# Windowed attention and rational hidden layer on one core: the early part written anew

## The chip, the cores and the metric

The kernel runs on 1 core of one Trainium2 chip. The metric is the time of one execution on the device in microseconds (us); the time before is the median of three runs.

## The reference

```python
def _attn_ref(x, weight_gen):            # x 4 x 4096 x 192, weight_gen 4 x 4096 x 8 x 7
    w = weight_gen - np.max(weight_gen, axis=-1, keepdims=True)
    w = np.exp(w)
    w = w / (np.sum(w, axis=-1, keepdims=True) + 1e-09)
    ...
    out = np.einsum('bshk,bskhg->bshg', w, x_unf)

def _moe_ref(x, w_in, w_out, a, b):      # w_in 192 x 2048, w_out 2048 x 192
    h = x @ w_in
    h2 = h * h
    h3 = h2 * h
    P = a[0] + a[1] * h + a[2] * h2 + a[3] * h3
    Q = 1.0 + np.abs(b[0]) * np.abs(h) + np.abs(b[1]) * h2
    g = P / (Q + 1e-06)
    return (g @ w_out).astype(np.float32)
```

Each token has, for each of 8 heads, seven softmaxed weights over itself and the six tokens before it (the taps). The weighted sum, 192 wide, goes through a hidden layer of 2048 with the rational function g = P/Q. The inputs `w_in` and `w_out` come as 64-bit numbers, which the kernel rounds to 32 bits itself.

## The kernel before

The 16384 tokens are cut into 32 chunks of 512 (128 partitions, 4 tokens each). A chunk is prepared: loads of the gates and of x (`lg`, `lx`), the softmax (L509 to L534), seven taps, each a product x times weight (L560) with a sum, four or six transposes on PE (`tr`), a rounding to the product's number format (`cast`, ScalarE), the residue of that rounding (`rest`, VectorE), and copies with the partitions' halves swapped by DMA (`both`, xd L680 and xs L686). For all chunks but the first, POOL multiplies and adds the taps (L560, L572, L578). For chunk 0 (`early`) VectorE multiplies all seven, PE adds them in PSUM by products with an identity (`fold`, L596), ScalarE and VectorE copy the sum out (`settle` L603, `again` L608), and xs alone comes by DMA.

A chunk then has 8 slots of 256 hidden numbers each, 256 slots in all, counted through. A slot is: `m1`, the product on PE into an `h` tile (L716, 18 matmuls of high and low parts of weights and tokens); `v1`, Abs, and `z1`, Square of it on ScalarE (L750, L754); `d1` and `w1` on VectorE (L758, L762), the denominator and a factor of the numerator; `ln` and `ex` on ScalarE (L767, L770), which together invert the denominator; `gg` on VectorE (L774); and `m2` on PE, the sum over hidden numbers into the chunk's output tile `acc`, in two halves of 8 matmuls (L729; rows of the trace count 16, since each appears as two parts). Between the halves stands `relay`, an empty instruction on SP (L791): the second half waits for it, and it for the end of the first. After a chunk's last slot ScalarE copies `acc` out (L829) and SP issues the store (L832). There is one `acc`, so the next chunk's first half waits for that copy.

The weights come in 14 units (A0 to A3 and B0, B1 of `w_in`, W0 to W7 of `w_out`): a DMA (`ul`), an Abs of the high words and a rounding of the low words on ScalarE (`ua1` L397, `ua2` L401), four operations on VectorE that put the 32-bit number together (`ub1` to `ub4`, L406 to L421), of which the last sets to zero what is smaller in size than `TINY`; for A and B also a rounding on ScalarE and its residue on VectorE (`uh` L449, `uw` L452). Slot i of chunk 0 or 1 needs A(i//2), B(i//4) for its product and Wi for its sum.

The coefficients a and b come by two broadcast DMAs on ScalarE's queue (L264, L265); POOL, ScalarE and VectorE work two roots out of them (L279, L285 to L296), `powers` and `vertex` the numbers that the slots use. `judge` (POOL) tests the bounds within which this form of g may be used; if `slow` comes out as 1, the kernel computes all once more by `whole`. 30 products of the identity with itself (L274, `warm`) stand at the start of PE.

The order on each engine is not that of the code: every step is an `Op` with an engine, a duration, a key and what it needs, and `arrange` plays the schedule through and puts the instruction that can start with the smallest key next. Keys are due times, slot number times `PITCH` plus offsets `OFF` by kind of step, and `KEY` for the weight units.

```python
    def due(n):
        return START + PITCH * n
...
        o_d = op("DVE", 1.28, end - OFF["d"], d1, [o_v], uses=[AV], lock=True)
```

## Time and profile before

| | us |
|---|---|
| median of 3 runs (lowest, highest) | 1295.23 (1294.98, 1295.98) |
| profiled execution, its own time | 1295.15 |
| its span | 1293.4 |
| PE matmul busy in the span | 1249.6 (97%) |
| PEld, weight load of PE | 1150.7 (89%) |
| DVE (VectorE) | 1135.3 (88%) |
| ACT (ScalarE) | 1130.5 (87%) |
| POOL (GpSimd) | 883.1 (68%) |

The span goes from the first to the last recorded instruction; what lies around it is 1.75 us here. PEld overlaps PE. SP (SyncE) issues DMAs and relays and has no busy time of its own. A shape such as 128x1024 is partitions by elements. A row by stretch gives the engines in the order PE, PEld, DVE, ACT, POOL, then the clock granted to PE as a share of full speed, the DMA engines' busy share and GB/s.

### The profile page before, as it was taken

How to read it: one execution, taken by the hardware profiler on the slowest of the kernel's cores; microseconds unless marked ns; L12 is line 12 of the kernel's file. 1: busy time of each engine (PE TensorE's matmuls, PEld its weight loads, DVE VectorE, ACT ScalarE, POOL GpSimd, SP SyncE). 2: the span in 40 equal slices, each digit the busy share in tenths (PEclk: the TensorE clock that was granted, in tenths of full speed). 3: DMA queues.
4: the chain of work that ended last, by engine and by line, in shares of the span. 5: the costliest groups of instructions: out<-in, count | busy, mean ns of one | idle time of the engine just before them, and what ended most of it. 6: DMA issues, size and time to landing. Idle time of an engine off the chain costs nothing.

```text
span 1293.4 us, 31029 instructions
## 1 busy us (share of the span) xinstructions
PE 1249.6 (97%) x13268; PEld 1150.7 (89%) x13268; DVE 1135.3 (88%) x979; ACT 1130.5 (87%) x1162; POOL 883.1 (68%) x578
## 2 busy tenths in 40 slices
...
DMA packets 46293, 89.11 MB, mean 69 GB/s; under 512 B 5426, under 2 KB 27976, under 8 KB 46148
## 3 DMA queue, kind: packets, MB, share of 16 engines
...
q8 instruction: 106, 1.74, 0.5%
...
## 4 chain that ended last, share of the span: by engine, by line
PE 84%; DVE 5%; ACT 4%; POOL 3%; issue 2%; SPq 1%; DMA 1%; DVEq 0%; ACTq 0%; POOLq 0%
PE acc L729 47%; PE h L716 37%; ACT av L750 1%; DMA x<-in_x_dram 1%; ACT av L767 1%; DVE av L758 1%; POOL at L572 1%; ACT av L770 1%; DVE g L774 1%; POOL pr L560 1%; ACT pv L754 1%; PE h L644 1%; SPq L686 1%; SPq L680 0%; DVE h L411 0%
## 5 line engine op out<-in xcount | busy, mean ns | idle before, releaser
L729 PE MATMUL acc<-wo,g 64*128 64x192 f32 x8192 | 721.9, 324 | 13.5 <-DVE g L774 5.4
L729 PEld LDWEIGHTS acc<-wo,g 64*128 64x128 f32 x8192 | 683.9, 187 | 37.4 <-SPq L791 12.0
L758 DVE SCALAR_TENSOR_TENSOR av<-av,cf 128x1024 f32<-128x1024 f32 x256 | 422.5, 1650 | 97.6 <-ACT av L750 97.0
L572 POOL TENSOR_TENSOR at<-at,pr 128x768 f32<-128x768 f32 x155 | 362.9, 2341 | 12.0
L774 DVE SCALAR_TENSOR_TENSOR g<-h,ab,av 128x1024 f32<-128x1024 f32 x256 | 326.8, 1276 | 31.5 <-ACT av L770 22.5
L750 ACT ACTIVATE av<-h 128x1024 f32<-128x1024 f32 x256 | 260.9, 1019 | 83.3 <-PE h L716 82.5
L560 POOL TENSOR_TENSOR pr<-x,wn 128x768 f32<-128x768 f32 x186 | 332.7, 1789 | 0.1
L762 DVE SCALAR_TENSOR_TENSOR h<-pv,cf,h 128x1024 f32<-128x1024 f32 x256 | 326.3, 1274 | 2.2 <-ACT pv L754 2.2
L767 ACT ACTIVATE av<-av,c 128x1024 f32<-128x1024 f32 x256 | 294.1, 1149 | 32.3 <-DVE av L758 31.3
L754 ACT ACTIVATE pv<-h,cf,rt 128x1024 f32<-128x1024 f32 x256 | 307.7, 1202 | 0.0
L770 ACT ACTIVATE av<-av 128x1024 f32<-128x1024 f32 x256 | 270.6, 1057 | 2.8
L716 PE MATMUL h<-xm,wh 64*128 64x512 f32 x1024 | 242.1, 461 | 16.2 <-DVE g L774 13.8
L716 PE MATMUL h<-xs,wh 64*128 64x512 f32 x1024 | 208.9, 394 | 1.6 <-DMA xs<-xm 1.6
L716 PE MATMUL h<-xd,wh 64*128 64x512 f32 x1024 | 208.2, 394 | 0.0
L716 PEld LDWEIGHTS h<-xm,wh 64*128 64x128 f32 x1024 | 102.3, 188 | 27.7 <-issue 6.9
L716 PEld LDWEIGHTS h<-xs,wh 64*128 64x128 f32 x1024 | 102.6, 187 | 21.5 <-DMA xs<-xm 2.9
L716 PEld LDWEIGHTS h<-xd,wh 64*128 64x128 f32 x1024 | 102.0, 187 | 18.7
L513 POOL TENSOR_TENSOR e<-wgt,mx 128x224 f32<-128x224 f32 x31 | 20.9, 674 | 140.0 <-DVE mx L509 127.1
L716 PE MATMUL h<-xs,wl 64*128 64x512 f32 x512 | 104.2, 393 | 0.0
L716 PE MATMUL h<-xd,wl 64*128 64x512 f32 x512 | 103.9, 393 | 0.0
L716 PE MATMUL h<-xm,wl 64*128 64x512 f32 x512 | 103.9, 393 | 0.0
L578 POOL TENSOR_TENSOR as<-at,pr 128x512 f32<-128x512 f32 (+1 forms) x62 | 84.4, 1379 | 2.3
...
## 6 DMA issues: line engine op xcount, KB each, us to landing
...
```

What stands on the lines that cost most here:

```text
L560: eng.tensor_tensor(dst.rearrange("p q (h g) -> p q h g", g=G), t["x"][:, k:k + Q, :].rearrange("p q (h g) -> p q h g", g=G), t["wn"][:, k ...
L572: eng.tensor_tensor(at, at, term, op=ALU.add)
L578: eng.tensor_tensor(t["as"][:, start:start + Q * (hi - lo)].rearrange("p (q d) -> p q d", q=Q), at[:, :, lo:hi], term[:, :, lo:hi], op=ALU ...
L716: nc.tensor.matmul(h[:, f, :], w[half, b_, i, :], v[half, part, 0:N], start=k == 0, stop=k == 8, skip_group_check=True)
L729: done.append(nc.tensor.matmul(acc[:, bank, q_ * D:(q_ + 1) * D], g[half, f, seat(q) * P:(seat(q) + 1) * P], wo[half, 2 * i + f, :], start ...
L750: nc.scalar.activation(out=t["v"], in_=flat(t["h"]), func=ACTF.Abs)
L754: nc.scalar.activation(out=t["z"], in_=flat(t["h"]), func=ACTF.Square, scale=steep, bias=shift)
L758: nc.vector.scalar_tensor_tensor(out=t["v"], in0=t["v"], scalar=rb, in1=t["v"], op0=ALU.add, op1=ALU.mult)
L762: nc.vector.scalar_tensor_tensor(out=flat(t["h"]), in0=t["z"], scalar=lift, in1=flat(t["h"]), op0=ALU.add, op1=ALU.mult)
L767: nc.scalar.activation(out=t["v"], in_=t["v"], func=ACTF.Ln, bias=c0)
L770: nc.scalar.activation(out=t["v"], in_=t["v"], func=ACTF.Exp, scale=-1.0)
L774: nc.vector.scalar_tensor_tensor(out=flat(t["g"]), in0=flat(t["h"]), scalar=a0, in1=t["v"], op0=ALU.add, op1=ALU.mult)
```

## The change

- **Weight mask.** The units lose the Abs on ScalarE (`ua1`) and the masking on VectorE (`ub4`). Instead each unit is loaded a second time later (`verify`, from slot 40 on, one unit per chunk): an Abs on ScalarE, a compare-and-multiply and a maximum on VectorE. At the end one maximum over all goes to `slow`; if any weight is small and not zero, `whole` follows, after the weights have been masked as before (`refill`).
- **Squares on ScalarE.** For slots 0 to 6 (`SQUARED`) the step `d1`, v(v + rb) on VectorE, becomes (v + rb/2) squared on ScalarE (`q1`, in place), with the constant put right in the bias of `ln`. `judge` has a further bound on rb/2.
- **Swapped copy of chunk 0.** xs comes from four more transposes, a rounding and a residue (`trs`, `casts`, `rests`) in place of a DMA.
- **Taps of chunk 0.** The fifth and sixth are multiplied and summed on POOL (`few`, `pair`, `join`), the other five on VectorE; x is issued before the first weights.
- **Coefficients.** They come to one partition by two short DMAs and are spread by a product with a row of ones (`spread`) and a copy.
- **Dummy products.** 24 in place of 30 at the start, and `fill` puts groups of them in gaps of over 1.2 us that the planner sees on PE before 75 us; each group waits for one vector or scalar operation (`after`). The groups hold 52 in all.
- **Planner.** New numbers in `OFF`, `KEY`, `PITCH`, `PATIENCE`, `LOCK`, and with them another order on all engines over the whole program.

ScalarE where the first slots begin; `av`, `pv` and `h` are tiles of a slot, `cf` and `c` coefficients, `raw` and `rnd` belong to a weight unit. L750 is now L907, L754 L911, L767 L927, L770 L931; L919 is `q1`. Before:

```order
L750 ACTIVATE av<-h 128x1024
L754 ACTIVATE pv<-h,cf,rt 128x1024
L750 ACTIVATE av<-h 128x1024
L767 ACTIVATE av<-av,c_68 128x1024
L770 ACTIVATE av<-av 128x1024
L754 ACTIVATE pv<-h,cf,rt 128x1024
L767 ACTIVATE av<-av,c_68 128x1024
L770 ACTIVATE av<-av 128x1024
```

And now:

```order
L907 ACTIVATE av<-h 128x1024
L911 ACTIVATE pv<-h,cf,rt 128x1024
L907 ACTIVATE av<-h 128x1024
L911 ACTIVATE pv<-h,cf,rt 128x1024
L919 ACTIVATE av<-av,cf 128x1024
L927 ACTIVATE av<-av,cf 128x1024
L931 ACTIVATE av<-av 128x1024
L466 ACTIVATE rnd<-raw 128x512
L466 ACTIVATE rnd<-raw 128x384
L919 ACTIVATE av<-av,cf 128x1024
L927 ACTIVATE av<-av,cf 128x1024
L931 ACTIVATE av<-av 128x1024
```

The `ln` of slot 0 (L927) now follows a square on the same engine where it followed a step of VectorE, and two roundings of weights (L466, before L401) have moved between the two slots.

VectorE around the taps of chunk 0 (L560, now L666), with weight operations L406 to L421 (now L471 to L482). Before:

```order
L406 TENSOR_SCALAR h<-raw 128x512
L411 SCALAR_TENSOR_TENSOR h<-raw,h 128x512
L416 ISA h<-h,rnd 128x1024
L560 TENSOR_TENSOR pr<-x,h 128x768 x4
L406 TENSOR_SCALAR h<-raw 128x512
L560 TENSOR_TENSOR pr<-x,h 128x768 x2
L421 SCALAR_TENSOR_TENSOR h<-mag,h 128x512
L560 TENSOR_TENSOR pr<-x,h 128x768
```

And now:

```order
L347 RECIPROCAL tt<-rt 128x1
L348 SCALAR_TENSOR_TENSOR rt<-tt,sq,rt 128x1
L350 TENSOR_SCALAR rt<-rt 128x1
L351 RECIPROCAL tt<-rt 128x1
L666 TENSOR_TENSOR pr<-x,h 128x768 x4
L471 TENSOR_SCALAR h<-raw 128x512
L476 SCALAR_TENSOR_TENSOR h<-raw,h 128x512
L482 ISA h<-h,rnd 128x1024
L666 TENSOR_TENSOR pr<-x,h 128x768
L505 TENSOR_TENSOR wl<-h,wh 128x512
```

The second root's four operations (L347 to L351) now stand ahead of the taps, and the first weight unit's behind four of them.

PE where chunk 4 begins (slot 32): `acc` is a chunk's output tile, `wo` the output weights, `g` a slot's values, and L716 (now L873) the product of one slot. Before:

```order
L729 MATMUL acc_2311<-wo_71,g_2219 128x192 x8
L716 MATMUL h_2326<-xm_1867,wh_69 128x512 x2
L716 MATMUL h_2326<-xm_1867,wl_70 128x512 x2
L716 MATMUL h_2326<-xm_1867,wh_69 128x512 x2
L716 MATMUL h_2326<-xd_1900,wh_69 128x512 x2
L716 MATMUL h_2326<-xd_1900,wl_70 128x512 x2
L716 MATMUL h_2326<-xd_1900,wh_69 128x512 x2
L716 MATMUL h_2326<-xs_1905,wh_69 128x512 x2
L716 MATMUL h_2326<-xs_1905,wl_70 128x512 x2
L716 MATMUL h_2326<-xs_1905,wh_69 128x512 x2
L729 MATMUL acc_2311<-wo_71,g_2219 128x192 x8
L729 MATMUL acc_2311<-wo_71,g_2261 128x192 x8
```

And now:

```order
L886 MATMUL acc_1897<-wo_75,g_2168 128x192 x8
L873 MATMUL h_2363<-xm_1939,wh_73 128x512 x2
L873 MATMUL h_2363<-xm_1939,wl_74 128x512 x2
L873 MATMUL h_2363<-xm_1939,wh_73 128x512 x2
L873 MATMUL h_2363<-xd_1974,wh_73 128x512 x2
L873 MATMUL h_2363<-xd_1974,wl_74 128x512 x2
L873 MATMUL h_2363<-xd_1974,wh_73 128x512 x2
L873 MATMUL h_2363<-xs_1979,wh_73 128x512 x2
L873 MATMUL h_2363<-xs_1979,wl_74 128x512 x2
L873 MATMUL h_2363<-xs_1979,wh_73 128x512 x2
L886 MATMUL acc_2388<-wo_75,g_2219 128x192 x16
L886 MATMUL acc_2388<-wo_75,g_2272 128x192 x8
```

The product before stood between the two halves of the new chunk's first slot (acc_2311, g_2219); it now stands between the old chunk's last half (acc_1897) and the first of the new, and the two halves of that slot, x16, follow each other as a pair.

The diff, cut to its core (left out: the number tables, helpers that only moved, the second computation):

```diff
+CHECKED = 40
+SQUARED = 7
...
-PATIENCE = 0.302
+PATIENCE = 0.222
...
+def fill(order, filler):
+    done, last = [], None
+    gates = [o for o in order if o.eng in ("DVE", "ACT") and o.start < FILLED]
+    at = {o: i for i, o in enumerate(order)}
+    extra = {}
+    for o in order:
+        if o.eng != "PE":
+            continue
+        if last is not None and o.start < FILLED and o.start - last.end > 1.2:
+            until = last.end
+            for d in sorted((d for d in gates if last.end - 0.4 < d.end < o.start - 0.5),
+                            key=lambda d: d.end):
+                if d.fn.__name__ in GATES and d.end >= until:
+                    later = [x.end for x in gates if d.end + 0.5 < x.end < o.start - 0.3
+                             and x.fn.__name__ in GATES]
+                    room = min(later + [o.start - 0.3]) - d.end
+                    count = max(1, int(SHARE * room / 0.12))
+                    extra.setdefault(max(at[d], at[last]), []).append(
+                        Op("PE", 0.0, 0.0, filler(count, d)))
+                    until = d.end + 0.12 * count
+        last = o
+    for i, o in enumerate(order):
+        done.append(o)
+        done.extend(extra.get(i, ()))
+    return done
...
+SHARE = 0.5
+GATES = (
+    "ub1", "ub2", "ub3", "uw", "uh", "d1", "w1", "gg", "v1", "z1", "q1", "ln", "ex", "ua2",
+    "rests", "casts",
+)
+FILLED = 75.0
 LAP = {"ACT": 0.09, "DVE": 0.08, "POOL": 0.05}
-LOCK = 2.59
+LOCK = 5.16
...
     def load_ab():
-        nc.scalar.dma_start(out=ab[:, 0:4], in_=a.partition_broadcast(P))
-        nc.scalar.dma_start(out=ab[:, 4:6], in_=b.partition_broadcast(P))
-
-    o_ab = op("ACT", 0.9, -300.0, load_ab, land=4.0)
+        nc.scalar.dma_start(out=six[:, 0:4], in_=a.rearrange("(o n) -> o n", o=1))
+        nc.scalar.dma_start(out=six[:, 4:6], in_=b.rearrange("(o n) -> o n", o=1))
+
+    def spread():
+        T["spare"] = tiled(("acc", "warm"), [P, 2, N])
+        nc.tensor.matmul(T["spare"][:, 1, 0:6], one, six, start=True, stop=True)
+
+    o_one = op("DVE", 0.1, -400.0, lambda: nc.vector.memset(one, 1.0))
+    o_ab = op("ACT", 0.9, -300.0, load_ab, land=1.0)
+    o_six = op("PE", 0.2, -300.0, spread, [o_ab, o_one], takes=[("acc", "warm")])
+    o_ab = op("ACT", 0.2, -89.0, lambda: nc.scalar.copy(out=ab, in_=T["spare"][:, 1, 0:6]), [o_six],
+              uses=[("acc", "warm")])
...
+        out=mg, in_=T["spare"][:, 1, 0:6], func=ACTF.Abs), [o_six], uses=[("acc", "warm")])
+
+    def warm():
+        for k in range(WARM):
+            nc.tensor.matmul(T["spare"][:, 0, N - P:N], ident, ident, start=True, stop=True)
+
+    op("PE", 0.16 * WARM, -9.0, warm, [o_id, o_ab, o_mg], uses=[("acc", "warm")])
...
+        g.tensor_scalar(half_rb, rb, 0.5, None, op0=ALU.mult)
+        g.tensor_tensor(floor_, half_rb, half_rb, op=ALU.mult)
+        g.tensor_scalar(floor_, floor_, -1.0, 1.0 + 1e-6, op0=ALU.mult, op1=ALU.add)
...
+            (mg[:, 5:6], 2.0 ** -16, 2.0 ** 10), (half_rb, 0.0, 2.0),
...
-        def ua1():
-            t["mag"] = tiled(("mag", u), [P, width])
-            nc.scalar.activation(out=t["mag"], in_=t["hi"].bitcast(FP32), func=ACTF.Abs)
...
         def ub3():
-            nc.vector.tensor_tensor(t["w"], t["w"], t["rnd"], op=ALU.add)
-
-        def ub4():
-            w = t["w"]
-            dst = wo_flat[:, j * 2 * D:(j + 1) * 2 * D] if kind == "W" else w.bitcast(FP32)
-            nc.vector.scalar_tensor_tensor(
-                out=dst, in0=t["mag"], scalar=TINY, in1=w.bitcast(FP32), op0=ALU.is_ge,
-                op1=ALU.mult)
+            dst = wo_flat[:, j * 2 * D:(j + 1) * 2 * D].bitcast(I32) if kind == "W" else t["w"]
+            return nc.vector.tensor_tensor(dst, t["w"], t["rnd"], op=ALU.add)
...
+    def verify(k, u):
+        width, t = size_of(u), {}
+        cost = width / U
+        raw, mag, rnd = ((kind, ("again", u)) for kind in ("raw", "mag", "rnd"))
+        at = due(CHECKED + NS * k)
+
+        def load():
+            t["hi"], _ = fetch(u, tiled(raw, [P, 2, N]))
+
+        def size():
+            t["mag"] = tiled(mag, [P, width])
+            nc.scalar.activation(out=t["mag"], in_=t["hi"].bitcast(FP32), func=ACTF.Abs)
+
+        def small():
+            t["bad"] = tiled(rnd, [P, width], I32).bitcast(FP32)
+            nc.vector.scalar_tensor_tensor(
+                out=t["bad"], in0=t["mag"], scalar=TINY, in1=t["mag"], op0=ALU.is_lt, op1=ALU.mult)
+
+        def most():
+            nc.vector.tensor_reduce(out=worst[:, k:k + 1], in_=t["bad"], axis=AXX, op=ALU.max)
+
+        o = op("SP", 0.9, at, load, takes=[raw], land=512.0 * cost, after=at)
+        o = op("ACT", 0.67 * cost, at + OFF["vs"], size, [o], takes=[mag], uses=[raw])
+        o = op("DVE", 0.69 * cost, at + OFF["vs"], small, [o], takes=[rnd], uses=[mag], lock=True)
+        return op("DVE", 0.6 * cost, at + OFF["vs"], most, [o], uses=[rnd])
...
+    o_verified = [verify(k, u) for k, u in enumerate(LOADS)]
...
+    def verdict():
+        g = nc.gpsimd
+        t0, ok = cf[0:1, 13:14], cf[0:1, 14:15]
+        g.tensor_scalar(t0, worst[0:1, 0:1], 0.0, None, op0=ALU.is_le)
+        g.tensor_tensor(ok, ok, t0, op=ALU.mult)
+        g.tensor_scalar(slow, ok, -1.0, 1.0, op0=ALU.mult, op1=ALU.add)
...
+            def few():
+                t["few"] = tiled(("wn", c), [P, K, QH])
+                nc.gpsimd.tensor_tensor(
+                    t["few"][:, K - 2:K, :].rearrange("p k n -> p n k"), t["e"][:, :, K - 2:K],
+                    t["mx"].to_broadcast([P, QH, 2]), op=ALU.mult)
+
+            def pair(k):
+                def run():
+                    t["pr", k] = tiled(("at", (c, k)), [P, Q, D])
+                    nc.gpsimd.tensor_tensor(
+                        t["pr", k].rearrange("p q (h g) -> p q h g", g=G),
+                        t["x"][:, k:k + Q, :].rearrange("p q (h g) -> p q h g", g=G),
+                        t["few"][:, k, :].rearrange("p (q h) -> p q h", h=H).unsqueeze(3)
+                        .to_broadcast([P, Q, H, G]),
+                        op=ALU.mult)
+                return run
+
+            def join():
+                nc.gpsimd.tensor_tensor(t["pr", K - 1], t["pr", K - 1], t["pr", K - 2], op=ALU.add)
+
+            A5, A6 = (("at", (c, k)) for k in (K - 2, K - 1))
+            o = op("POOL", 0.3, k0 - 1, few, [o_mx], takes=[("wn", c)], uses=[E, MX])
+            o = op("POOL", 1.49, k0, pair(K - 2), [o, o_lx], takes=[A5], uses=[X, ("wn", c)])
+            o = op("POOL", 1.49, k0, pair(K - 1), [o, o_lz], takes=[A6], uses=[X, ("wn", c)])
+            o_join = op("POOL", 1.83, k0, join, [o], uses=[A5, A6])
...
         def settle():
-            t["at"] = tiled(AT, [P, 2 * N]).rearrange("p (q d) -> p q d", q=Q)
+            room = tiled(AT, [P, Q + HALO, D]).rearrange("p q d -> p (q d)")
+            t["at"] = room[:, 0:5 * Q * D2].rearrange("p (q d) -> p q d", q=Q)
             nc.scalar.copy(
-                out=t["at"][:, :, 0:D].rearrange("p (f q) d -> p f q d", f=2),
+                out=t["at"][:, :, D2:D2 + D].rearrange("p (f q) d -> p f q d", f=2),
                 in_=t["sum"][:, :, 0:2 * D].rearrange("p f (q d) -> p f q d", d=D))
 
         def again():
-            nc.vector.tensor_copy(
-                out=t["at"][:, :, D:2 * P].rearrange("p (f q) d -> p f q d", f=2),
-                in_=t["sum"][:, :, 0:2 * D].rearrange("p f (q d) -> p f q d", d=D)[:, :, :, P:D])
+            parts = t["at"].rearrange("p q (j d) -> p q j d", d=D2)
+            nc.vector.tensor_copy(out=parts[:, :, 0:5:4, :], in_=parts[:, :, 2:4, :])
...
+        def trs():
+            ps = t["px"] = tiled(TX, [P, 2, N])
+            for q in range(Q):
+                cols = slice(seat(q) * P, (seat(q) + 1) * P)
+                nc.tensor.transpose(ps[:, 0, cols], t["at"][:, q, 0:P], ident)
+
+        def casts():
+            t["xs"] = tiled(XS, [P, 2, N], FP32R)
+            return nc.scalar.copy(out=t["xs"][:, 0, :], in_=t["px"][:, 0, :])
+
+        def rests():
+            return nc.vector.tensor_tensor(
+                t["xs"][:, 1, :], t["px"][:, 0, :], t["xs"][:, 0, :].bitcast(FP32),
+                op=ALU.subtract)
...
-        o_both = op("SP", 0.9 if early else 2.7, tkey, both, [o_cast, o_rest],
-                    takes=[XS] if early else [XD, XS], uses=[XM], land=512.0 if early else 1024.0)
+        if early:
+            o = op("PE", 0.6, tkey + 0.5, trs, [o_tr], takes=[TX], uses=[AT])
+            o_casts = op("ACT", 0.6, tkey + OFF["cast"] + 0.5, casts, [o], takes=[XS], uses=[TX])
+            o_rests = op("DVE", 0.7, tkey + OFF["rest"] + 0.5, rests, [o_casts], uses=[TX, XS])
+            return t, [o_cast, o_rest, o_casts, o_rests], [XM, XD, XS], o_tr
+        o_both = op("SP", 4.4, tkey, both, [o_cast, o_rest], takes=[XD, XS], uses=[XM], land=1024.0)
...
+        def q1():
+            return nc.scalar.activation(out=t["v"], in_=t["v"], func=ACTF.Square, bias=half_rb)
...
-            nc.scalar.activation(out=t["v"], in_=t["v"], func=ACTF.Ln, bias=c0)
+            return nc.scalar.activation(
+                out=t["v"], in_=t["v"], func=ACTF.Ln, bias=floor_ if n < SQUARED else c0)
...
-        o_d = op("DVE", 1.28, end - OFF["d"], d1, [o_v], uses=[AV], lock=True)
+        if n < SQUARED:
+            o_d = op("ACT", 1.15, end - OFF["sq"], q1, [o_v], uses=[AV])
+        else:
+            o_d = op("DVE", 1.28, end - OFF["d"], d1, [o_v], uses=[AV], lock=True)
...
+    def filler(count, gate):
+        def run():
+            for k in range(count):
+                dummy = nc.tensor.matmul(
+                    T["spare"][:, 0, N - P:N], ident, ident, start=False, stop=True,
+                    skip_group_check=True)
+                if not k:
+                    after(dummy, made_by[gate])
+        return run
+
+    order = fill(arrange(ops, place), filler)
     with tc.manual_schedule():
         nc.scalar.preload_act_table_set("natural_log_exp_and_others")
         for o in order:
-            o.fn()
+            made_by[o] = o.fn()
...
+        for u in LOADS:
+            refill(u)
...
-WARM = 30
-DVE_TAPS = (0, 1, 2, 3, 4, 5, 6)
+WARM = 24
```

## Rows read from the trace of the kernel before

**Rows 1.** Busy time by stretch: length, busy us (instructions) by engine, granted clock, DMA

```profile
25.00:85.00 60.00, 37.50 (x270) 30.30 (x271) 54.95 (x72) 40.06 (x52) 49.41 (x34) 0.75 0.39 106
...
60.00:65.00 5.00, 0.51 (x8) 0.21 (x4) 4.86 (x8) 2.87 (x5) 4.92 (x4) 1.00 0.44 95
...
900.00:1200.00 300.00, 299.14 (x3246) 275.11 (x3244) 272.81 (x224) 274.14 (x278) 222.19 (x134) 1.00 0.25 69
```

**Rows 2.** Timeline, early: start, us, engine, line, operation, count, [idle before <-releaser]

```profile
2.54 9.13 PE L274 MATMUL acc<-ident 128*128 128x128 f32 x60 [2.54 <-POOL ident masks.py:199]
...
6.03 0.21 ACT L279 ACTIVATE mg<-ab 128x6 f32<-128x6 f32 x1 [4.01 <-DMA ab<-in_moe_b_dram]
...
35.65 1.03 ACT L750 ACTIVATE av<-h 128x1024 f32<-128x1024 f32 x1
...
36.55 1.22 ACT L754 ACTIVATE pv<-h,cf,rt 128x1024 f32<-128x1024 f32 x1
...
85.75 1.48 PE L729 MATMUL acc<-wo,g 64*128 64x192 f32 x16
```

**Rows 3.** Chain of waits that ended last, first 110 us: start, us, what

```profile
3.55 8.45 DMA x<-in_x_dram
...
12.09 0.97 DVE pr L560
...
65.92 2.93 PE acc L729 x16
...
81.87 4.05 PE h L716 x18
...
85.92 1.30 PE acc L729 x16
...
87.22 2.05 PE h L716 x18
```

**Rows 4.** Groups by line and shape, whole span: busy us, mean ns, idle before

```profile
L560 DVE TENSOR_TENSOR pr<-x,h 128x768 f32<-128x768 f32 x7 | 6.4, 950 | 0.4 <-DMA x<-in_x_dram 0.2 <-PE h L596 0.2
...
L411 DVE SCALAR_TENSOR_TENSOR h<-raw,h 128x512 int32<-128x512 int32 x6 | 4.1, 688 | 0.1
...
L411 DVE SCALAR_TENSOR_TENSOR h<-raw,h 128x384 int32<-128x384 int32 x8 | 4.5, 560 | 0.2
...
L758 DVE SCALAR_TENSOR_TENSOR av<-av,cf 128x1024 f32<-128x1024 f32 x256 | 422.5, 1650 | 97.6 <-ACT av L750 97.0
...
L750 ACT ACTIVATE av<-h 128x1024 f32<-128x1024 f32 x256 | 260.9, 1019 | 83.3 <-PE h L716 82.5
...
L754 ACT ACTIVATE pv<-h,cf,rt 128x1024 f32<-128x1024 f32 x256 | 307.7, 1202 | 0.0
...
L767 ACT ACTIVATE av<-av,c 128x1024 f32<-128x1024 f32 x256 | 294.1, 1149 | 32.3 <-DVE av L758 31.3
...
L770 ACT ACTIVATE av<-av 128x1024 f32<-128x1024 f32 x256 | 270.6, 1057 | 2.8
...
L401 ACT ACTIVATE rnd<-raw 128x512 int32<-128x512 uint32 x6 | 4.1, 678 | 6.9 <-DMA raw<-in_moe_w_in_dram 4.5 <-DVE h L416 2.4
```

**Rows 5.** Timeline, VectorE and POOL, 608 to 616 us

```profile
610.52 2.96 DVE L758 SCALAR_TENSOR_TENSOR av<-av,cf 128x1024 f32<-128x1024 f32 x1
...
614.59 1.31 DVE L758 SCALAR_TENSOR_TENSOR av<-av,cf 128x1024 f32<-128x1024 f32 x1
...
610.55 1.84 POOL L572 TENSOR_TENSOR at<-at,pr 128x768 f32<-128x768 f32 x1
```

**Rows 6.** Timeline, PE, at the sums of slots 24 and 40

```profile
187.66 4.79 PE L729 MATMUL acc<-wo,g 64*128 64x192 f32 x32 [2.13 <-ACT ob L829]
...
270.76 2.87 PE L729 MATMUL acc<-wo,g 64*128 64x192 f32 x32 [1.74 <-SPq L791]
```

**Rows 7.** Chain of waits that ended last, its tail

```profile
1274.37 2.90 PE acc L729 x32
...
1277.34 2.90 PE acc L729 x32
```

228 lines of the change are left out of this document (138 added, 90 removed).

## The prediction

> **What bounds the kernel now.** I read the stretches of time first, then the chain of waits, the groups by shape, and the timeline where a date was needed. In the stretch from 900 to 1200 us PE is busy 299.14 of 300 us at full clock, VectorE and ScalarE about 273 each [rows 1]. There the kernel is a row of products and weighted sums on PE, and whatever the others do fits beside it. The stretch from 25 to 85 us reads otherwise: VectorE 54.95 of 60, PE 37.50, at a mean granted clock of 0.75 [rows 1]. So there are two regimes: at first VectorE sets the pace, and PE catches up later. What is worth anything in the early part is how soon PE gets into its unbroken row; from there its work is fixed.
>
> Two marks measure that: ScalarE begins the first Abs of slot 0 (`v1`) at 35.65, and PE begins the output sum of slot 4 at 85.75 [rows 2]. The clock matters as well: in the stretch from 60 to 65 PE was busy 0.51 of 5 us, and the half sum behind it took 2.93, against 1.30 for one at 85.92; a product took 4.05 at one place and 2.05 at the next [rows 1, 3]. The slow ones are at the 1.2 GHz level, the others at 2.4.
>
> **The change part by part.**
>
> *First mark.* Before, the first tap began at 12.09, when the x load had landed [rows 3]. Now x is issued ahead of the first weight block, so the load is out of the way; but the second root's vector operations stand ahead of the taps, and they wait on POOL's chain from the coefficients. Before, ScalarE had those at 6.03, after an idle 4.01 [rows 2]. They now come as one row, through a product and two copies. This path has no row: 2 us earlier if the short load takes half of that idle time, 0.7 later if the new hops and three more POOL operations count in full. I take 12.1, as before.
>
> From there VectorE's order up to the last weight word that the first Abs waits for (through a ScalarE cast ahead of it) holds 5 taps at 0.95, 14 operations of 512 columns at 0.69 (words, low parts, and the three residues), 4 of 384 columns at 0.56, and four small ones, some 0.4 each (an estimate) [rows 4]: 4.75 + 9.66 + 2.24 + 1.5 = 18.15. Two casts of at most 0.68, what a rounding of that width takes, stand in that path, less the overlap of one operation with the next: 1.1 for both. 12.1 + 18.15 + 1.1 puts the first Abs at 31.4, against 35.65. The PE side is ready by then, because the swapped copy no longer comes by DMA but by four transposes, a cast and a residue (both counted).
>
> *Second mark.* The d1 step of slots 0 to 6 leaves VectorE, where one cost 1.65 on average, and becomes a Square on ScalarE. In-place Square has no row; between the Abs at 1.02 and the Square from PSUM at 1.20 I take 1.15 [rows 4]. The mask's two operations per weight unit go as well: 14 on VectorE, 14 on ScalarE, at 0.69 and 0.56 by width (about 8.6 and 8.4 us). With both gone VectorE is no longer the longest; ScalarE's order from the first Abs to the Square of slot 5 is. It holds 6 Abs (6.11), 6 Squares (7.21), 5 new Squares (5.75), 5 Ln (5.75), 5 Exp (5.29), 7 weight roundings (4.75 at the width of 512; four are narrower), two casts (1.2) and two small ones (1.2, an estimate): 37.25 [rows 4]. Successive operations overlap by about 0.1 where they don't depend on each other (35.65 plus 1.03 ends after 36.55, where the next begins [rows 2]); 27 of the 37 joins do that, and the others cost 0.03 each: 34.9. That ends at 66.3. Then VectorE's w1 of slot 5 (1.28), a low part (0.69) and five weight operations of 384 columns (2.8) stand before the output weights of slot 4 are ready: 71.1. I add 0.6 for one hole on ScalarE, where slot 4's product waits for its weights (0 to 3.5, a unit's five operations). So slot 4's sum begins at 71.7 instead of 85.75, a gain of 14.05. From there PE's order holds the same work as before, and I carry the gain unchanged.
>
> *The seven slots on ScalarE, the two taps and their sum on POOL, the memset:* counted above, or beside it. POOL is idle there before; its sum is wanted after the fifth tap.
>
> *Dummy products.* 52 of them, released by vector and scalar operations, stand in gaps of PE. On PE they cost nothing while the marks are set by ScalarE and VectorE; if that cover goes, 0.3 each at the lower clock, as the 30 warm-up products took 9.13 [rows 2]: 16 in all.
>
> *Later test.* One unit per chunk, 14 chunks: two weight loads on SP's queue, an Abs on ScalarE (0.68), two operations on VectorE (0.69 and 0.6). Per chunk of 38 us VectorE has 3.5 us idle (27 us in 300 [rows 1]), ScalarE about as much: zero on the path. Rows speak of one thing more: d1 of one late slot took 2.96 while POOL's add of 1.84 ran, and the next 1.31 [rows 5]. The test's comparison reads two SBUF operands too, so it can wait up to 1.7 us: 3.0 per chunk, still under 3.5. The Trainium skill, "SBUF — State Buffer", section "Who interferes with whom", says that a VectorE instruction with two SBUF inputs and a GpSimd instruction that reads SBUF exclude each other, the first to start holding the port to its end. That speaks against the test, and would make the sum 14 times 3.0 of VectorE time; the row of 2.96 agrees with it, and the idle time covers it.
>
> *PE's order later on.* This is what the change costs. The two halves of a slot's sum are joined by a relay on SP. Where a product stands between them the relay is hidden; where they follow each other, PE waits. In the tail, where every slot is such a pair, one takes 2.97 (1274.37 to 1277.34) against two halves of 1.30 [rows 3, 7]: 0.37 more, of which I put 0.3 on the pair, since the step to the next slot is slower there too. Between slot 15 and slot 239 the new order has 31 such pairs, the old one 3, two of which are in the losses below: 30 × 0.3 = +9.0. The losses of the old order go, as the chunks' beginnings are ordered anew: at 187.66 PE waited 2.13 for the copy of the old sums and then ran 32 matmuls in 4.79 at the lower clock instead of 2.60, 4.3 together; at 270.76 it waited 1.74 for SP behind its DMA issues, 2.0 with the pair [rows 6]: −6.3. The new chunk beginnings put one product between the last old sum and the first new one; that covers the copy of 0.8 mostly: +1.5 over 25 chunks (an estimate; 0 to 5).
>
> **Sum:** −14.05 + 9.0 − 6.3 + 1.5 = −9.85. The profiled execution took 1295.15 us (span 1293.4), 0.08 under the median of 1295.23. So 1285.3; I say 1285.5 us, 0.75% faster. A measurement of this kernel can tell about 0.2%, 2.6 us, from no change.
>
> **Rivals.** *Relays behind DMA issues (slower).* The relay is one of SP's instructions, in order with its DMA issues, and the change adds two issues per tested unit. At 270.76 one pair met the issues and paid 1.74 [rows 6]. If every second of the 31 pairs does, that is 16 × 1.74 = 28, and the time 1313. It decides from a mean of 0.6 per pair, where the 30 pairs eat the whole gain. For it: pairs are now where chunks begin, and there SP issues copies and the output store. Against: of the two old pairs that stood near a chunk's beginning, only one paid this, and the new ones come after the store is issued, which itself waits for the copy that the pair waits for. Chance 0.10.
>
> *The clock stays low in the early part.* If the dummies don't hold it, slot 0, 1 and 4's products and a half sum run at 4.05 and 2.93 and come late to ScalarE: three times 2.0 and 1.6, 7.6, and 1293. For it: the clock was at the lower level in about half of the time from 25 to 85, as after a stretch with 0.51 us of work in 5 [rows 1, 3]. Against: the products of slots 0 and 1 are no longer interrupted by a DMA, and dummies stand in each later gap. [...] Chance 0.10, with 1289 to 1294.
>
> *The change does not do what it says:* the fast path is left, because the new bounds on the coefficients or the weight test trip, and all is computed a second time: over 2500 us. Nothing in the trace speaks for it; chance 0.02.
>
> **How the numbers follow.** The forecast has 0.78, all of it faster. Half of the clock's 0.10 lies inside 0.2%, half is faster; relays and slow path are slower. Faster 0.83, same 0.05, slower 0.12. The range: the first tap 2 us earlier, no hole, no wait for the copies and a pair at 0.25 take off 5.6 and reach down to 1280; a hole of 3.5, a tap 0.7 later and pairs at 0.37 add 5.7, and a clock that falls once makes it 1292. That holds 0.8; the rest lies mostly above.
>
> **What would show it.** The first Abs of slot 0 near 31, the first sum of slot 4 near 72, ScalarE almost without idle time between them; a granted clock near 1 from 40 us on; pairs at chunk beginnings 0.3 us longer than a slot's two halves; no wait of PE over 1 us after 110; VectorE over 93% in the middle. I am wrong if slot 4's sum begins after 80, or if PE's waits for SP add up to over 15 us.

## The result, and the profile after

The changed kernel takes 1283.61 us (four runs, 1283.33 to 1284.14) against 1295.61 before (four runs, 1294.98 to 1296.27): the ratio is 0.9908, with a 95% interval of 0.9891 to 0.9925. The forecast was 1285.5, between 1280 and 1292. The profiled execution's span is 1282.0, 11.4 less than before.

First the stretches of time, which answer [rows 1] (core 0: length, PE, PEld, DVE, ACT, POOL busy with counts, granted clock, DMA share, GB/s):

```profile
25.00:35.00 10.00, 9.24 (x74) 8.03 (x75) 8.41 (x14) 7.17 (x10) 6.61 (x6) 1.00 0.65 163
35.00:42.00 7.00, 6.84 (x58) 5.99 (x57) 4.77 (x7) 6.90 (x8) 6.84 (x5) 1.00 0.52 171
...
60.00:65.00 5.00, 4.89 (x54) 4.21 (x52) 3.76 (x6) 4.93 (x6) 4.92 (x4) 1.00 0.71 159
...
25.00:85.00 60.00, 55.30 (x512) 48.06 (x514) 50.55 (x66) 55.02 (x64) 46.47 (x34) 1.00 0.41 114
...
900.00:1200.00 300.00, 298.96 (x3219) 276.43 (x3216) 267.64 (x216) 270.56 (x273) 229.30 (x132) 1.00 0.24 65
```

From 25 to 85 us PE is busy 55.30 instead of 37.50, at the full clock instead of 0.75, though some of that is dummies; VectorE is down from 54.95 to 50.55, and ScalarE is up from 40.06 to 55.02 and now the longest of the three others. In the late stretch PE is as full as before by this count: 298.96 of 300.

The timeline of the early part, which answers [rows 2, 3] (start, busy, engine, line, operation, tiles, count, idle before and its releaser):

```profile
3.51 0.18 ACT L329 ACTIVATE mg<-acc 128x6 f32<-128x6 f32 x1 [1.49 <-PE acc L318]
...
10.19 0.16 DVE L351 RECIPROCAL tt<-rt 128x1 f32<-128x1 f32 x1
10.27 2.68 DVE L666 TENSOR_TENSOR pr<-x,h 128x768 f32<-128x768 f32 x3
...
29.49 1.03 ACT L907 ACTIVATE av<-h 128x1024 f32<-128x1024 f32 x1
...
48.54 1.57 PE L886 MATMUL acc<-wo,g 64*128 64x192 f32 x16 [1.44 <-SPq L952]
...
55.29 1.02 ACT L907 ACTIVATE av<-h 128x1024 f32<-128x1024 f32 x1 [0.96 <-PE h L873]
...
63.45 1.20 ACT L911 ACTIVATE pv<-h,cf,rt 128x1024 f32<-128x1024 f32 x1
...
69.69 1.57 PE L886 MATMUL acc<-wo,g 64*128 64x192 f32 x16 [0.99 <-DVE wo L482]
```

ScalarE has the coefficients at 3.51 (6.03 before), the first tap begins at 10.27 (12.09), the first Abs at 29.49 (35.65), slot 4's sum at 69.69 (85.75). To follow the gain through the program, the table gives the beginning of a slot's first half sum in both timelines, and how many products PE had begun by then:

| slot | before, us (products) | after, us (products) | earlier by |
|---|---|---|---|
| 4 | 85.75 (7) | 69.69 (7) | 16.06 |
| 15 | 142.05 (19) | 125.93 (19) | 16.12 |
| 44 | 286.25 (48) | 268.90 (49) | 17.35, and one product more |
| 228 | 1161.92 (233) | 1149.83 (233) | 12.09 |
| 252 | 1275.77 (256) | 1263.26 (256) | 12.51 |

A product is 2.05 [rows 3], so at slot 44 the kernel is some 19.4 ahead; by slot 228 it has given 7.3 of that back. Between slot 252 and the end 1.1 more goes, all of it behind the last store. There SP reads `slow` and jumps over the second computation; its next recorded instruction comes 3.9 after the store's issue (1280.1 after 1276.19), before 2.8 (1291.5 after 1288.70). The changed kernel's second computation is longer by `refill`, and from slot 255's sum to the end every run built on the changed kernel takes 9.4 to 9.8, with or without the later test, where the kernel before and the one run built on it take 8.7. What in the longer program costs this was not tried.

### The profile page after: what moved, and what is told of

Read it like the earlier page. It is cut to its first block, busy times and chain, and to the rows that moved or that the text cites. A ratio compares the mean times of both kernels' runs of the same rounds, so it can differ in the third digit from the quotient of the medians.

```text
span 1282.0 us, 31077 instructions
## 1 busy us (share of the span) xinstructions
PE 1259.6 (98%) x13362; PEld 1160.6 (91%) x13362; DVE 1142.8 (89%) x988; ACT 1139.5 (89%) x1171; POOL 908.4 (71%) x591
## 4 chain that ended last, share of the span: by engine, by line
PE 87%; ACT 5%; POOL 2%; DVE 2%; issue 1%; SPq 1%; DMA 0%; ACTq 0%; DVEq 0%; POOLq 0%
PE acc L886 48%; PE h L873 38%; ACT av L927 1%; ACT pv L911 1%; ACT av L907 1%; ACT av L931 1%; POOL at L678 1%; PE h L783 1%; PE acc L334 1%; POOL pr L666 1%; DVE g L935 0%; DMA raw<-in_moe_w_in_dram 0%; ACT av L919 0%; DVE h L471 0%; SPq L818 0%
## 5 line engine op out<-in xcount | busy, mean ns | idle before, releaser
L666 POOL TENSOR_TENSOR pr<-x,wn 128x768 f32<-128x768 f32 x186 | 359.8, 1934 | 0.1
L678 POOL TENSOR_TENSOR at<-at,pr 128x768 f32<-128x768 f32 x155 | 348.5, 2248 | 11.8
L907 ACT ACTIVATE av<-h 128x1024 f32<-128x1024 f32 x256 | 260.5, 1018 | 71.8 <-PE h L873 70.5
L911 ACT ACTIVATE pv<-h,cf,rt 128x1024 f32<-128x1024 f32 x256 | 307.2, 1200 | 0.0
L927 ACT ACTIVATE av<-av,c 128x1024 f32<-128x1024 f32 x249 | 285.6, 1147 | 23.9 <-DVE av L915 23.0
L931 ACT ACTIVATE av<-av 128x1024 f32<-128x1024 f32 x256 | 270.3, 1056 | 3.8
L873 PE MATMUL h<-xm,wh 64*128 64x512 f32 x1024 | 237.3, 450 | 1.6 <-DVE g L935 1.4
L873 PE MATMUL h<-xd,wh 64*128 64x512 f32 x1024 | 207.7, 392 | 0.0
L873 PE MATMUL h<-xs,wh 64*128 64x512 f32 x1024 | 207.6, 391 | 0.0
L873 PEld LDWEIGHTS h<-xs,wh 64*128 64x128 f32 x1024 | 102.0, 185 | 16.5
L873 PEld LDWEIGHTS h<-xd,wh 64*128 64x128 f32 x1024 | 101.3, 184 | 17.1
L873 PEld LDWEIGHTS h<-xm,wh 64*128 64x128 f32 x1024 | 101.6, 185 | 13.0 <-DVE g L935 2.2
L629 POOL TENSOR_SCALAR mx<-mx,cf 128x32 f32<-128x32 f32 x31 | 12.0, 386 | 135.3 <-DVE mx L626 135.1
L873 PE MATMUL h<-xm,wl 64*128 64x512 f32 x512 | 103.1, 389 | 0.9 <-DVE wl L505 0.9
L873 PE MATMUL h<-xd,wl 64*128 64x512 f32 x512 | 103.2, 389 | 0.0
L873 PE MATMUL h<-xs,wl 64*128 64x512 f32 x512 | 102.9, 387 | 0.0
L684 POOL TENSOR_TENSOR as<-at,pr 128x512 f32<-128x512 f32 (+1 forms) x62 | 79.7, 1300 | 2.0
```

Of the source, the lines that this page charges most:

```text
L666: eng.tensor_tensor(dst.rearrange("p q (h g) -> p q h g", g=G), t["x"][:, k:k + Q, :].rearrange("p q (h g) -> p q h g", g=G), t["wn"][:, k ...
L678: eng.tensor_tensor(at, at, term, op=ALU.add)
L684: eng.tensor_tensor(t["as"][:, start:start + Q * (hi - lo)].rearrange("p (q d) -> p q d", q=Q), at[:, :, lo:hi], term[:, :, lo:hi], op=ALU ...
L873: nc.tensor.matmul(h[:, f, :], w[half, b_, i, :], v[half, part, 0:N], start=k == 0, stop=k == 8, skip_group_check=True)
L907: return nc.scalar.activation(out=t["v"], in_=flat(t["h"]), func=ACTF.Abs)
L911: return nc.scalar.activation(out=t["z"], in_=flat(t["h"]), func=ACTF.Square, scale=steep, bias=shift)
```

## The experiments

All are built on the changed kernel unless said otherwise, and each is compared with its 1283.61. Those that alter an operation are ordered anew by the planner, so their middle differs too. Slot 15 (125.93 in the changed kernel) lies ahead of the middle and is the mark used for the early part; it is not free of the order either, since other planner's numbers alone move it by 2.45 (below).

### The dummies

```diff
-    order = fill(arrange(ops, place), filler)
+    order = arrange(ops, place)
```

> The changed kernel without the 52 dummy products in PE's gaps (the 24 at the start stay); the order is otherwise the same. Theory: the dummies hold TensorE's clock, which was granted in full up to 1279 us with them; without them it falls in parts of the stretch from 30 to 70 us, as it did before the change, products there take 4.05 instead of 2.05 and half sums 2.93 instead of 1.30, the sum of slot 4 begins 4 to 10 us after 69.69, and the time is 1287 to 1293. Rival: the real products are close enough together now, the clock stays, and the time is 1283 to 1285 with the sum of slot 4 within 1 us of 69.7.

1284.21 (1283.81 to 1287.36). The rival holds for the time. The stretches of this run, in the same columns:

```profile
25.00:35.00 10.00, 4.40 (x36) 3.88 (x36) 7.86 (x13) 7.15 (x8) 7.32 (x7) 1.00 0.63 156
35.00:42.00 7.00, 4.40 (x22) 3.83 (x24) 5.12 (x6) 5.51 (x8) 6.84 (x5) 0.51 0.46 155
42.00:60.00 18.00, 13.31 (x140) 10.84 (x138) 15.73 (x22) 17.48 (x22) 12.76 (x12) 1.00 0.35 97
```

The clock did fall, to 0.51 between 35 and 42 us, after a stretch with 4.40 of 10 us of work; with dummies the same stretches read 9.24 and 1.00. It fell only once: from 42 to 60 us, with 13.31 of 18 us of work and no dummy, it reads 1.00. From the first Abs to slot 15's sum this kernel takes 97.76 (28.70 to 126.46) and the changed one 96.44 (29.49 to 125.93), so in this pair of profiles the dummies are worth 1.3 there.

That the first Abs comes 0.79 earlier here is not their doing: the difference is there before the first dummy of a gap stands on PE, at 21.10. The changed kernel's start has these rows:

```profile
3.88 8.36 PE L334 MATMUL acc<-ident 128*128 128x128 f32 x48 [0.41 <-ACT ab L323]
...
13.57 0.95 DVE L666 TENSOR_TENSOR pr<-x,h 128x768 f32<-128x768 f32 x1 [0.61 <-PE h L702]
```

And this run's:

```profile
3.77 7.54 PE L334 MATMUL acc<-ident 128*128 128x128 f32 x48 [0.41 <-ACT ab L323]
...
10.18 3.56 DVE L666 TENSOR_TENSOR pr<-x,h 128x768 f32<-128x768 f32 x4
```

The 24 products at the start are the same in both, but took 8.36 in one profiled execution and 7.54 in the other. PE's sum of the taps stands behind them; where they end late, the fourth tap on VectorE waits for it (0.61), and everything behind it on VectorE up to the first Abs is later by that. In all runs with 24 such products they took 7.04 to 8.54. So two profiles can differ by up to 0.9 at the first Abs for this reason alone.

One of the four runs took 1287.36, with a mean granted clock of 0.989 where the others have 0.996 and 0.997: it seems that the dummies buy steadiness, but four runs don't show that.

### Each part undone

Squares of slots 0 to 6 back on VectorE:

```diff
-SQUARED = 7
+SQUARED = 0
```

> The changed kernel with d1 of slots 0 to 6 back on VectorE (SQUARED 0). Theory: VectorE, busy 50.55 of the 60 us from 25 to 85 while ScalarE is busy 55.02, takes 7 times 1.28 to 1.71, some 9 to 12 us, back and becomes the longest again; the sums of slots 4 to 8 begin 4 to 9 us later and the time is 1288 to 1293. Rival: ScalarE is the longest in this part, so that taking 7 squares of 1.15 from it makes room and the time does not rise: 1279 to 1285.

1293.15 (1291.95 to 1295.60), 9.5 more: the theory, just above its range. VectorE is busy 55.56 from 25 to 85 us and ScalarE 42.30, almost the shares of before. The place was wrong: slot 4's sum begins at 68.42, but with 6 products begun where the changed kernel has 7 at 69.69; with a product at 2.05 that is only some 0.8 behind. The loss shows from slot 8 on (99.46 against 92.77, 12 products in both); at slot 15 it is 7.65. A part of it is the clock, which falls once here (0.96 on the mean from 85 to 130 us); but one of the runs had a mean clock of 1.000 and still took 1291.95.

The mask back in the weight units, the later test left out:

```diff
+        def ub4():
+            ...
+            return nc.vector.scalar_tensor_tensor(
+                out=dst, in0=t["mag"], scalar=TINY, in1=w.bitcast(FP32), op0=ALU.is_ge,
+                op1=ALU.mult)
...
+        p1 = op("ACT", 0.67 * cost, base, ua1, [o, p2], uses=[raw, mag])
...
-    o_verified = [verify(k, u) for k, u in enumerate(LOADS)]
```

> The changed kernel with the two mask operations back in each weight unit, and without the later test. Theory: 14 operations of 0.56 to 0.69 on each of VectorE and ScalarE, 8.6 and 8.4 us, lie on the two engines that set the early part, and come back almost whole: the sum of slot 4 begins 6 to 10 us later, and the time is 1289 to 1293, of which leaving out the test gives nothing back. Rival: they fit in holes of the two engines, of which ScalarE has under 3 us between 29.5 and 64.6 and VectorE more: 1283 to 1286. If the later test itself cost something in the middle, the time after slot 40 would run faster than in the changed kernel.

1295.50 (1295.04 to 1297.00), 11.9 more, the whole gain and more than the theory's 1293. Early it is what the theory says: slot 4's sum 7.2 later, slot 15's 7.35. Another 4.4 goes behind slot 15, and it is lost before slot 44, where no weight unit is left to do and the order is another. Whether the mask has a share in that was not separated.

The swapped copy by DMA:

```diff
+            o_both = op("SP", 0.9, tkey, swap, [o_cast, o_rest], takes=[XS], uses=[XM], land=512.0)
+            return t, [o_cast, o_rest, o_both], [XM, XD, XS], o_tr
```

> The changed kernel with the swapped copy of chunk 0 by DMA again, in place of four transposes, a rounding and a residue. Theory: the two DMAs start after the residue at about 27 and land some 6 us later, so the products of slots 0 and 1 end near 35 instead of 31.5 and the first Abs comes 4 to 6 us after 29.49; ScalarE, which has no idle time behind it, carries that to the end: 1287 to 1290. Rival: a rounding and a residue less on the two engines (1.3 us) and the weights' last words (at 30.3) cover it: 1282 to 1285.

1290.67 (1290.37 to 1291.18), 7.1 more, 7.08 of it at slot 15. The first Abs came at 38.32, 8.83 later, more than the theory's 4 to 6. The chain of waits of this run shows why:

```profile
24.89 11.12 PE acc L1025 x94
36.01 2.29 PE h L883 x18
38.30 0.02 issue
38.32 1.03 ACT av L917
```

The copies' DMAs were issued at 26.2 and 26.9 and landed 5.3 later, near 32.2; but the planner saw a long gap on PE and filled it with 49 dummies, whose last ended at 36.01. It counts a dummy as 0.12 us; these took 0.237 (11.12 for 47 of them). They held slot 0's product by up to 3.8, but not the first Abs: the planner had also put weight units into the gap, and ScalarE's cast ahead of the Abs waited for VectorE's word of one of them:

```profile
36.34 0.59 ACT L502 CAST wh<-h 128x512 fp32r<-128x512 f32 x1 [3.49 <-DVE h L482]
38.32 1.03 ACT L917 ACTIVATE av<-h 128x1024 f32<-128x1024 f32 x1 [1.40 <-PE h L883]
```

So at most 1.4 of the 8.8 is the dummies'; the rest is the DMA and the order made around it, which this run doesn't part.

The coefficients by broadcast:

```diff
-        nc.scalar.dma_start(out=six[:, 0:4], in_=a.rearrange("(o n) -> o n", o=1))
-        nc.scalar.dma_start(out=six[:, 4:6], in_=b.rearrange("(o n) -> o n", o=1))
+        nc.scalar.dma_start(out=ab[:, 0:4], in_=a.partition_broadcast(P))
+        nc.scalar.dma_start(out=ab[:, 4:6], in_=b.partition_broadcast(P))
```

> The changed kernel with the coefficients by two broadcast DMAs straight to all partitions, as before, instead of a short load, a product and a copy. Theory: the first tap waits for the second root (its last operation ended at 10.19, the tap began at 10.27), and that for the coefficients, which ScalarE had at 3.51 and would have at about 6.0: the first tap comes 1.5 to 2.5 us later, near 12.1, and all behind it: 1285 to 1286.5. Rival: the tap waits for x all the same, which before the change landed at 12.0 behind the first weights, or a hole later on takes it up: 1283.2 to 1284.4.

1287.59 (1287.22 to 1288.31), 4.0 more. The timeline of this run:

```profile
7.50 0.21 ACT L327 ACTIVATE mg<-ab 128x6 f32<-128x6 f32 x1 [5.48 <-DMA ab<-in_moe_b_dram]
...
13.64 0.17 DVE L349 RECIPROCAL tt<-rt 128x1 f32<-128x1 f32 x1
13.72 2.68 DVE L664 TENSOR_TENSOR pr<-x,h 128x768 f32<-128x768 f32 x3
```

The mechanism is the theory's, the size is not: the broadcasts now landed at 7.5 instead of 6.0, with the x load issued beside them. The first tap is 3.45 late, slot 15 is 3.48 late, slot 252 is 3.74 late. This is the cleanest sight of the early chain, for the order is the same (the products at the start alone begin earlier, at 2.54): what its head loses, the end loses.

All taps on VectorE:

```diff
-            o_join = op("POOL", 1.83, k0, join, [o], uses=[A5, A6])
...
-            if early and k == K - 2:
-                continue
```

> The changed kernel with all seven taps of chunk 0 multiplied on VectorE, none on POOL. Theory: the way to the first Abs runs through VectorE (it is busy 16.50 of the first 25 us, without a hole over 0.7 from 10.27 on), so two more products of 0.95 come back there and at the end: 1285 to 1286.5. Rival: POOL's sum ended at 16.33 and the fifth tap on VectorE, which waits behind a weight unit, at 17.55, so POOL's two taps replace work that fits into holes: 1283 to 1284.5.

1289.10 (1288.33 to 1289.54), 5.5 more. That is above both ranges. The theory accounts for slot 15, 2.14 later. By slot 128 only 0.8 of it is left (674.19 against 673.39), and by slot 244 it is 6.1 (1233.13 against 1227.07): that is lost where the taps of chunk 0 are long done and the order is another.

The earlier issue of x was not undone by itself. In the changed kernel x has landed by 7.2, before at 12.0; with x at 12.0 the first tap could not have begun at 10.27.

### One part alone

The kernel before, with the squares only:

```diff
+        if n < SQUARED:
+            o_d = op("ACT", 1.15, end + 6.43, q1, [o_v], uses=[AV])
+        else:
             o_d = op("DVE", 1.28, end - OFF["d"], d1, [o_v], uses=[AV], lock=True)
```

> The kernel before with one part of the change alone: d1 of slots 0 to 6 as a Square on ScalarE. Theory: the early part is a race of VectorE, ScalarE and PE, whose longest sets the end; before, VectorE was it with 54.95 of 60 us, so taking 7 times 1.65 from it moves the sum of slot 8 from 109.30 by 6 to 9 us and the time to 1286 to 1290, though undoing the same part of the change cost 9.5 there, where the other parts had made room. Rival: the parts add up, so that this one alone gives its 9.5 and more: under 1286; or the mask's operations still hold VectorE and it gives under 4: over 1291.

1290.37 (1288.95 to 1294.09) against 1295.18 before in this comparison: 4.8 less, a ratio of 0.9967 (0.9957 to 0.9978). Neither text had it right: the time lies between their ranges, and slot 8's sum is 2.84 ahead (106.46) where the theory had 6 to 9. At slot 15 it is 2.74 (139.31 against 142.05); the first Abs comes as late as before (35.56), and the masks are still on both engines. The rest came behind slot 15, in another order. Undone at slot 15, the parts cost 7.65, 7.35, 7.08, 3.48, 2.14 and 0.53, together 28.2, where the whole change gained 16.1; done alone, the squares gain 2.7. The parts don't add up, and the 0.9 by which profiles differ at the start and the 1.4 of dummies in one of the runs don't make up the difference. It looks as if each part takes away one of several chains of about the same length; the other parts were not tried alone.

### The later test

The test's instructions left out (the output is not guarded against small weights), all others in the same order:

```diff
         def load():
-            t["hi"], _ = fetch(u, tiled(raw, [P, 2, N]))
+            pass
```

> The changed kernel in the same order, but with the later test of the weights left out (28 loads, 14 Abs, 14 comparisons, 14 maxima, and the verdict's maximum). Theory: the test lies beside other work and costs nothing: 1283.0 to 1284.2. Rival: VectorE, at 282 of 300 us from 300 to 600, pays for it, 1.2 us per chunk and more where POOL holds a comparison up: up to 14 times 0.4, and the time falls to 1278 to 1282, between slots 40 and 152.

1283.32 (1283.05 to 1283.49), 0.3 less: the theory. In the profiles all of it is there at slot 15 (125.59 against 125.93), ahead of the test; from slot 15 to 252 this run takes 1137.60 and the changed kernel 1137.33. The test is covered.

### The middle: pairs and what stands in their place

One number, by which a second half goes ahead of a second product in a row:

```diff
-    "w1": 3.91, "m2": 6.44, "aft": 5.35, "step": 2.35, "cast": 2.11, "rest": -13.13, "dup": 12.47,
+    "w1": 3.91, "m2": 6.44, "aft": 5.2, "step": 2.35, "cast": 2.11, "rest": -13.13, "dup": 12.47,
```

> The changed kernel with one number of the planner, OFF aft, at 5.2 instead of 5.35, so that a slot's second half sum goes ahead of a second product in a row. Pairs (two halves of one slot with no product between) fall from 31 to 17 between slots 9 and 243; the early part is the same. Theory: a pair costs 0.39 (three halves in a row took 4.15 from 251.86 against 1.16 and twice 1.30), and pairs are what the middle loses: 14 times 0.39, so 1277 to 1280. Rival: the pairs stand where PE would wait anyway, since VectorE is busy 282 of 300 us there; without them PE waits for values of VectorE or for the copy of the sums, and the time is 1283 to 1290.

1284.79 (1284.53 to 1285.10), 1.2 more: the rival. Then the planner's numbers of before:

```diff
-PITCH = 4.8784
+PITCH = 4.8729
...
-    "w1": 3.91, "m2": 6.44, "aft": 5.35, "step": 2.35, "cast": 2.11, "rest": -13.13, "dup": 12.47,
+    "w1": 3.82, "m2": 3.16, "aft": 4.99, "step": 2.35, "cast": -1.03, "rest": -13.5, "dup": 13.03,
...
-PATIENCE = 0.222
+PATIENCE = 0.302
...
-LOCK = 5.16
+LOCK = 2.59
```

> The changed kernel with the planner's numbers of before (OFF, PITCH, PATIENCE, LOCK; KEY and START stay as changed). Six pairs in place of 31 between slots 9 and 243. Theory of the pairs: 25 times 0.39, 9.8, come back in the middle less what the old numbers lost at single places (1.7 to 2.1 us at a wait for the copy or for the relay behind DMA issues): 1274 to 1280. Rival: the numbers were fitted to this order of work, and the old ones bring waits of PE for VectorE that weigh more than the pairs: 1284 to 1292.

1281.10 (1279.46 to 1282.39), 2.5 less. That lies between the two texts, and where it was gained speaks for the rival: at slot 15 this kernel is already 2.45 ahead of the changed one (123.48), of which 0.60 is there at the first Abs (28.89) and is the start; at slot 252 it is 2.65 ahead (1260.61). The middle is worth the same with 6 pairs as with 31.

Yet a pair costs about what was said. The transposes of the next chunk stand once in each chunk, so their distance is a chunk's time. In the changed kernel, with one pair between each two of these rows:

```profile
317.77 0.54 PE L783 MATMUL h<-ident,as 64*128 64x64 f32 x12
...
356.05 0.54 PE L783 MATMUL h<-ident,as 64*128 64x64 f32 x12
...
394.28 0.54 PE L783 MATMUL h<-ident,as 64*128 64x64 f32 x12
```

And with the old numbers, where slot 48's pair lies between the first two rows and no pair after that:

```profile
277.00 0.53 PE L783 MATMUL h<-ident,as 64*128 64x64 f32 x12
...
315.23 0.54 PE L783 MATMUL h<-ident,as 64*128 64x64 f32 x12
...
353.14 0.54 PE L783 MATMUL h<-ident,as 64*128 64x64 f32 x12
...
391.00 0.54 PE L783 MATMUL h<-ident,as 64*128 64x64 f32 x12
```

With a pair 38.28, 38.23 and 38.23, without 37.91 and 37.86: 0.36 for a pair. What pays it back are waits. PE's largest in the changed kernel, apart from the first load (engine, line, what it waited for: total, times, longest):

```profile
PE acc L886 <- SPq L952: 2.0, 2, 1.4
PE h L873 <- DVE g L935: 1.4, 3, 0.5
PE acc L1015 <- DVE h L476: 1.3, 1, 1.3
```

With one number changed:

```profile
PE acc L886 <- ACT ob L993: 3.3, 2, 1.7
PE h L873 <- DVE g L935: 3.0, 5, 1.4
```

And with the old numbers:

```profile
PE acc L886 <- ACT ob L993: 3.3, 2, 1.7
...
PE h L873 <- DVE xm L809: 2.5, 3, 1.4
```

With one number changed, 14 pairs less are worth 5.0, and from slot 15 to 252 the kernel is yet 1.6 slower. Of the 6.6 to be found, 3.3 is the copy of the sums and 1.6 is VectorE's values; the rest was not put down to rows. With the old numbers the new waits that are listed make 5.8 of the 9.0 of 25 pairs; the rest was not put down to rows.

### A version that is faster than both

A third set of numbers:

```diff
-    "w1": 3.91, "m2": 6.44, "aft": 5.35, "step": 2.35, "cast": 2.11, "rest": -13.13, "dup": 12.47,
+    "w1": 3.82, "m2": 2.61, "aft": 6.15, "step": 2.67, "cast": -1.03, "rest": -13.85, "dup": 13.03,
...
-PATIENCE = 0.222
+PATIENCE = 0.2583
...
-LOCK = 5.16
+LOCK = 2.59
```

> The changed kernel with a third set of planner's numbers (near the old ones; LOCK 2.59, PATIENCE 0.258, m2 2.61, aft 6.15, PITCH 4.8767), under which 13 pairs stand between slots 9 and 243, against 31 as changed and 6 with the old numbers. Theory: a chunk without a pair takes 37.82 or 37.96 and one with a pair 38.18 or 38.33, so 18 pairs less are worth 6.6, and the time falls below that of the old numbers, 1281.1, where waits for the sums' copy (twice 1.7) and for VectorE stayed: 1275 to 1280. Rival: each pair that goes is paid back by a wait of PE for VectorE or ScalarE, as in the run with one number changed: 1280 to 1285.

1279.56 (1278.84 to 1280.72), 4.0 less than the change, inside the theory's range though near its upper end: 0.96 is there at slot 15, 3.61 at slot 252. Eighteen pairs less brought 2.65 in the middle, not 6.6. Then, on top of it, the dummies at their measured size:

```diff
-                    count = max(1, int(SHARE * room / 0.12))
+                    count = max(1, int(SHARE * room / 0.24))
...
-                    until = d.end + 0.12 * count
+                    until = d.end + 0.24 * count
```

> The kernel with the third set of numbers, and a dummy counted as 0.24 us instead of 0.12 where groups are filled in, so that 27 stand in PE's gaps after the start instead of 55 (27.5 us for 110 of them at 0.24 to 0.28 measured was too much for the gaps of 1 to 7 us). Theory: the twelve rows of dummies ahead of slot 0's product, 1.61 us from 25.80, held it back, as without dummies the first Abs came at 28.70 instead of 29.49; with half of them the first Abs comes 0.4 to 0.8 earlier than 29.72, the clock stays, and the time is 1278.6 to 1279.3. Rival: half the dummies don't hold the clock between 30 and 45 us, some products run at 4.05, and the time is 1279.5 to 1283, or spreads over more than 2 us.

1277.69 (1276.91 to 1278.66), against 1295.32 before in this comparison: a ratio of 0.9867 (0.9850 to 0.9883), the lowest median of all and below both texts. The first Abs is at 28.82 (29.72), and the clock stays, as its stretches show:

```profile
25.00:35.00 10.00, 8.33 (x58) 6.72 (x58) 7.98 (x13) 7.17 (x9) 7.19 (x7) 1.00 0.68 167
35.00:42.00 7.00, 5.87 (x48) 5.01 (x50) 5.13 (x6) 6.90 (x10) 6.92 (x5) 1.00 0.45 158
```

But little of this is the dummies'. The 0.9 at the first Abs is the start again: the 24 products took 7.56 here and 8.54 in the run before, where the fourth tap waited 0.79 behind them and here not at all. The expectation read 28.70 against 29.49 as the work of dummies, and it counted 110 of them, which are rows, two to a dummy. From the first Abs to slot 15 this kernel takes 94.74 (to 123.56) against 95.25 (to 124.97): 0.5 that half the dummies may be worth. Another 1.5 comes between slots 15 and 252, in the same order, and is not explained. The two ratios' intervals overlap (0.9850 to 0.9883 and 0.9863 to 0.9896), so that fewer dummies are faster is likely and not shown.

## Why the prediction was right

**First mark.** Right in its working, 1.9 too late in its result. From the first tap to the first Abs I had 19.3, and it is 19.22; the operations on VectorE are those that I counted, and the first Abs follows the cast that I named. The closeness is in part luck: 19.22 holds the fourth tap's wait of 0.61 for PE, which I had not, and in the run without dummies, where that wait is missing, it is 18.52 (10.18 to 28.70). The step that missed is "I take 12.1, as before" for the first tap: the short load brought the coefficients at 3.51 instead of 6.03, x had landed by 7.2, and the tap began at 10.27, near the end of the range I gave it (2 us earlier). The run with the broadcast shows that this head of the chain goes through to the end one for one.

**Second mark.** From the first Abs to the end of slot 5's Square I had 34.9, and 0.6 for one hole; it is 35.16 (29.49 to 64.65), with a hole of 0.96 at 55.29 in it. The new Square, which had no row, I took at 1.15; its group reads 1.149 in seven instances:

```profile
L919 ACT ACTIVATE av<-av,cf 128x1024 f32<-128x1024 f32 x7 | 8.0, 1149 | 0.0
```

From there to slot 4's sum I had 4.8, and it is 5.04. The cause of the hole is only in part the one I named, slot 4's product waiting for its weights. In the changed kernel the last of them was ready at 52.18, and the product began at 52.92, behind dummies:

```profile
50.04 2.94 PE L1015 MATMUL acc<-ident 128*128 128x128 f32 x24
...
51.49 0.69 DVE L505 TENSOR_TENSOR wl<-h,wh 128x512 fp32r<-128x512 f32 x1
```

Up to 0.74 of the 0.96 is theirs. In the run without dummies that product does wait for its weights:

```profile
52.93 0.50 PE L873 MATMUL h<-xm,wl 64*128 64x512 f32 x2 [0.82 <-DVE wl L505]
```

The first rival, a relay behind DMA issues, happened once early, at 48.54, for 1.44, ahead of a product whose weights were not ready before 52.18; after 100 us no wait of PE exceeds 0.5, so the rival fell. The whole of this mark's gain is 16.06 against the 14.05 forecast, and 1.83 of the difference is the first tap. Right too: from there the gain is carried (16.12 at slot 15).

The naming of the mark was the weak point. Slot 4's sum is not where the early part ends: with the squares undone it is late by only some 0.8, counted in products, and slot 15's by 7.65. I carried the gain from slot 4 on because PE's order holds the same work behind it; that run shows that the same work can still come 6.9 later.

**The later order.** I had 9.0 for pairs, 6.3 back from the old losses, 1.5 for the copies: 4.2 in all. Measured from slot 4 to slot 252 it is 3.55 (16.06 less 12.51), but three of the terms are off. A pair is 0.36, not 0.3, which makes 1.8 more on 30 of them; the 0.37 that I read in the tail was nearer than what I took from it. The old losses between slots 15 and 44 came back less fully: 3.3 net (16.12 to 19.4), 4.7 with the four pairs in that stretch counted out, against 6.3. And the 1.5 for the copies is not there: behind 100 us no wait of PE for a copy is listed in the changed kernel. With these the sum would be 6.1. What makes up for it is mostly what the old kernel lost behind slot 44 and I left out: five more waits of PE for a relay, 3.1 in all, the longest 1.2 at 1224.15. So the total is near because errors cancel, which is luck. The 1.1 behind the last store I did not have at all.

**Dummies.** I wrote that they cost nothing on PE while others set the marks. At the first Abs that holds; at the hole of 55.29 they cost up to 0.74. The rival of the low clock had them in its condition, "if the dummies don't hold it"; they held it, but without them the real work lost 1.0 from the first Abs to slot 4's sum (41.20 against 40.20) and 1.3 to slot 15's, not 7.6. The Trainium skill, "TensorE: Matmul & The Clock Gate", section "What's actually happening", calls the slow clock the default, which activity releases: the run without dummies agrees (0.51 after 4.40 of 10 us of work), and so does the changed kernel (1.00 after 9.24 of 10).

**The later test, the fast path.** Covered, as forecast (0.3), and the second computation was not entered. I had reckoned with comparisons held up by POOL, 1.7 us each; none was:

```profile
L526 DVE SCALAR_TENSOR_TENSOR rnd<-mag 128x512 f32<-128x512 f32 x6 | 4.1, 681 | 0.0
```

The mean is that of an operation of 512 columns without any wait. The Trainium skill, "SBUF — State Buffer", section "Who interferes with whom", lets such an instruction and one of GpSimd that reads SBUF exclude each other. These rows hardly test it: 9 of the 14 comparisons stand where POOL does nothing, and in the other five POOL was in its last 0.1 us or began after the comparison had, so that none had to give way to it. Whether the planner's `lock` brought that about wasn't tried.
